# A gated FNet kernel on one core: the last four units of its final product, the sum of its last quarter, one weight of MLP1 and the side jobs of ten MLP1 units in another order

## The chip, the cores and the metric

One core of a Trainium2 chip runs the whole program. The metric is the device time of one execution in microseconds (us), the median of several; lower is better.

## The reference

The input x has 2048 tokens of 512 features; all values are float32.

```
xn  = layernorm(x)                                  # over the 512 features
a,b = xn @ Wd_re^T, xn @ Wd_im^T                    # DFT over the features
s   = Ws_re @ a - Ws_im @ b                         # DFT over the tokens, real part
h   = relu(xn @ w1 + b1) ** 2                       # 512 -> 1792   (MLP1)
g   = silu(h @ w2 + b2)                             # 1792 -> 512   (MLP2)
out = x + s * g
```

## The kernel before

**Arithmetic.** Each float32 matrix is split into a high and a low part (`split`): ScalarE writes the high part as float32r (`split_hi`, L125), VectorE subtracts it from the value and writes the low part (`split_lo`, L128). A product is three matmuls: high by high, high by low, low by high (`PASSES`). Most large products also use a Winograd-Strassen scheme: a 2x2 block product is made of seven products, numbered 1 to 7 (`PRODUCTS`), of sums of blocks. VectorE makes the sums (`sums_b`, L257 to L259; `sums_a`, L263 to L269). "C11, C12, C21, C22" are the four quarters of a result; quarter C21 is the combination that needs product 4 and the sum of the others.

**Stages, in the order of TensorE's queue.** (1) The DFT over the tokens, `PQD = ct^T xn`, in eight chunks of 256 columns, each of eight steps j (L340 for the first two chunks, L325 after). (2) The DFT over the features, eight `YUnit`s (L705), whose operands are read back from DRAM. (3) MLP1, 28 `HUnit`s (L705): unit n has token group c = n // 7 (512 tokens) and weight p = n % 7 (256 hidden features). Its result goes to DRAM (`HD`). (4) MLP2, the units n = 0 to 27 again (`outer`, L811): each adds its share to seven PSUM banks, one for each Strassen product (eight for the last token group, where product 4 has one bank for each half of its columns, `m4[0]` and `m4[1]`). After seven units a token group is combined (`combine`, or by hand for the last group), passed through silu, multiplied by s, added to x and written.

**Order.** Everything is scheduled by hand: each engine runs its instructions in the order in which the program lists them. The work beside the matmuls (loading, summing and splitting operands) is cut into jobs, generators whose next step is issued by `go("name")`. The tables say where: `EARLY[(chunk, step)]` in stage 1, `Y_SIDE` in stage 2, `H_SIDE[n]` in stage 3 with three places in a unit, `O_SIDE` in stage 4. In a unit of stage 3, `before` is the unit ahead of it:

```
go(*first); unit.products(1); seed; before.c11(); before.products(5); before.c22()
before.products(4); before.c21(); go(*second); unit.products(7); unit.m7()
unit.products(6); seed; before.products(3); before.c12(); unit.products(2)
before.square(); go(*later)
```

`c22` and `c21` are on VectorE (L775, or L715 and L718 in the units of `ACT_PAIR`, with L790 after them in the other units), so a job in `first` stands ahead of them on VectorE and one in `second` behind them. Product 3 of a unit is added in the PSUM region that its `c22` has read ("B"), so these matmuls wait for `c22`.

**Jobs by their letters.** V: a weight of MLP1, loaded, summed and split in stages 2 and 3 (`make_w1`, three steps: load, sums, split). v: the same made during stage 1 and written to DRAM (`weight`, four steps: load, sums, then twice split-and-store), for the weights in `W1_EARLY`. k: such a weight read back (`load_w1`, two steps, one for each of the high and low parts, 896 KB each). w: a weight of MLP2 (`make_w2`; load, sums, split). x: a token block (`tokens`), m: its row statistics (`load_rows`). h: an operand of stage 4 (`operand`: load, sums, split). y: an early operand of stage 2 (`y_early`). p: a weight of stage 2 read back (`load_wd`). d: the weights of stage 2 made.

**Buffers that matter here.** `wd0` holds in turn a weight of stage 2, weight 6 of MLP1 (`W1_HOME`) and, in stage 4, the raw operands of every fourth unit. `pq00`, `pq01` are scratch for the v and y jobs with an even number. `u` has three buffers. The split operands of stage 4 rotate over `xc6`, `xc7`, `xc4`.

**The end (L1028 to L1074).** `REST = NP - 3`: the last three units (25, 26, 27) are not added product by product in the loop but kept for the end, where the order of products is chosen so that the quarters of the last token group come ready one after the other. `step` combines a bank with a quarter (L1039), `silu` is ScalarE (L854), `times` multiplies by s (L858), `plus` adds x and issues the store (L863, L864). The last quarter is C21: when the last bank `m4[1]` is complete, `step` subtracts it from the sum of the others, then silu, `times`, `plus` and the store follow. `finish` for an earlier token group may let a GpSimd DMA add x from DRAM (L846), with `put` (L849) as the store.

Of the kernel before, what the change touches and what calls it, by code (L numbers as in the profile page):

```python
# [9 lines left out]
F32R = mybir.dt.float32r  # L10
AF = mybir.ActivationFunctionType
ALU = mybir.AluOpType

P = 128
S, D, F = 2048, 512, 1792
NS, ND, NF = S // P, D // P, F // P
NJ, NP = NS // 2, NF // 2
# [3 lines left out]
NTC = S // TC  # L21
# [2 lines left out]

ASIDE = 4.2

REST = NP - 3

W1_EARLY = (0, 1)
W2_LATE = (4, 5)  # L30


EARLY = {
# [7 lines left out]
}  # L41
# [13 lines left out]

H_SIDE = {
    0: ((), ("V2", "x2"), ("x3",)),
    1: (("V4",), ("V3",), ("V5",)),
    2: ((), ("V4", "V5"), ("V6",)),
    3: ((), ("x3", "V5"), ("m2",)),  # L60
    4: ((), ("V6", "x2"), ("x4",)),
    5: ((), ("V6", "x3"), ("w4",)),
    6: ((), ("x3",), ("x5",)),
    7: (("w4",), ("w4",), ("w5",)),
    8: ((), ("x4",), ()),
# [10 lines left out]
    21: (("h1",), (), ()),  # L76
    22: (("w1",), ("h0",), ("w2",)),
    23: ((), ("h1",), ("w3",)),
    24: (("w2",), ("w1",), ("w6", "h2")),
    25: (("w3",), ("w2",), ("h3", "l4")),  # L80
    26: (("w6",), ("w3",), ("l5",)),
    27: (("h2",), (), ()),
}
ACT_PAIR = (7, 10, 13, 15, 17, 18, 19, 20, 26)
O_SIDE = {0: (("h4",), ("h5",)), 1: ((), ("w6",))}
# [28 lines left out]
C21, C11, C22, C12 = range(4)  # L114
# [5 lines left out]
def fnet_gated_kernel(ctx, tc, x, xt, ct, wd, w1, w2, b1, b2, out):  # L120
    nc = tc.nc
# [27 lines left out]
    WDD = [dram.tile([P, 2, 7, 256], F32, name=f"wdd{n}") for n in range(ND)]  # L149
    W1D = {p: dram.tile([P, 2, 7, 256], F32, name=f"w1d{p}") for p in W1_EARLY}  # L150
    W2D = {p: dram.tile([P, 2, 7, 256], F32, name=f"w2d{p}") for p in W2_LATE}
# [3 lines left out]
    def bank(tag, name):  # L155

        return acc.tile([P, 512], F32, tag=tag, name=name)

    def buf(tag, shape, name, dtype=F32):
        bufs = {"u": 3, "bn": 3, "sm": 3}.get(tag, 1)  # L160
        return pool.tile(shape, dtype, tag=tag, bufs=bufs, name=name)
# [86 lines left out]
    def plain_parts(c, j, hs=slice(0, 2)):  # L248
        if (c, j) not in part:
            part[c, j] = buf("g" + "ab"[j % 2], [P, 2, 4, CW], f"g{c}_{j}", F32R)  # L250
        g, r = part[c, j], raw[c, j]
        s = slice(2 * hs.start, 2 * hs.stop)
        return g[:, HI, s], g[:, LO, s], r[:, s]
# [21 lines left out]
    def sums_w1(t, r):  # L275
        sums_a(t, r[:, 0:1], r[:, 1:4:2], r[:, 1], r[:, 2], turned=True)
# [67 lines left out]
    one, two = slice(0, 1), slice(1, 2)  # L344
# [38 lines left out]

    Y_HOME = ("xc2", "xc3"), ("xc4", "xc5"), ("xc6", "xc7")
    YFIRST = 3
    yop, yraw, WDP = {}, {}, []

    def y_load(n):
        if n < 2 * NC:
# [25 lines left out]

    def load_wd(n):
        t = buf(("wd0", "wd1", "xc0", "xc1")[n], [P, 2, 7, 256], f"wdp{n}", F32R)
        WDP.append(t)
        for i in range(2):
            nc.sync.dma_start(t[:, i].bitcast(F32), WDD[n][:, i])  # L420
            yield
# [35 lines left out]
    g = plain_parts(0, 1)  # L457
# [7 lines left out]
    for j in range(1, NJ):  # L465
# [15 lines left out]
        g = plain_parts(*order[j + 1])  # L481
# [62 lines left out]
    for n, s in enumerate(steps):  # L544
        c, j = s
        if j == 0:
            ms = {k: bank(tag, f"m{k}_{c}") for k, tag in
                  {1: "bb", 2: "b20", 6: "b21", 3: "b30", 5: "b31", 7: "b32", 4: ("ba", "bc")[c % 2]}.items()}
        g = part.pop(s)
# [22 lines left out]
        if j == NJ - 1:  # L572
            e = buf("e", [P, 2048], f"c{c}")
# [9 lines left out]
    xT, W1, W2, fin, ready = {}, {}, {}, {}, {}  # L583
# [52 lines left out]
        yield  # L636

    def make_w1(p):
        e = buf({4: "e", 6: "e"}.get(p, "u"), [P, 8, 256], f"w1raw{p}")
        nc.sync.dma_start(e[:, 0:4], w1[p])  # L640
        yield
        sums_w1(e[:, 4:8], e)
        yield
        t = W1[p] = buf(W1_HOME[p], [P, 2, 7, 256], f"w1_{p}", F32R)
        split(t[:, HI], t[:, LO], e[:, 1:8])
        yield
# [20 lines left out]
    def operand(n):  # L667

        apart = n in (0, 1, 3)
        if apart:  # L670
            x_, t = (buf(f"pq{n % 3}{i}", [P, 4, 256], f"hr{n}_{i}") for i in range(2))
        else:
            e = buf("u" if n % 4 else "wd0", [P, 8, 256], f"hr{n}")
            x_, t = e[:, 4:8], e[:, 0:4]
        nc.sync.dma_start(x_, HD[divmod(n, NP)])
        yield
        sums_rows(t, x_)
        yield
        g = ready[n] = buf(("xc6", "xc7", "xc4")[n % 3], [P, 2, 7, 256], f"g{n}", F32R)
        for s, src in ((slice(0, 4), t), (slice(4, 7), x_[:, 0:3])) if apart else ((slice(0, 7), e[:, 0:7]),):  # L680
            split(g[:, HI, s], g[:, LO, s], src)
        yield
# [122 lines left out]
    def outer(m, k, n, cols=(0, 1)):  # L805

        p = n % NP
        a, b = PRODUCTS[k]
        for i in cols:
            for a_, b_ in PASSES:  # L810
                nc.tensor.matmul(m[:, i * 256:(i + 1) * 256], ready[n][:, a_, H_SLOT[a], i * P:(i + 1) * P],  # L811
                                 W2[p][:, b_, b], start=p == 0 and i == 0 and (a_, b_) == (HI, HI) and k not in BIASED,
                                 stop=p == NP - 1 and (a_, b_) == (LO, HI), skip_group_check=True)
# [22 lines left out]
    def finish(c, e, k):  # L836

        if len(fin[c]) > 2 + k // 2:
            silu(e, k)
            times(c, e, k)  # L840
            plus(c, e, k)
            return
        silu(e, k)
        times(c, e, k)
        z = e[:, k].rearrange("p (k e) -> p k e", e=256)
        nc.gpsimd.dma_start(z, at(x[c * TC:(c + 1) * TC], k), accum_op=ALU.add)  # L846

    def put(c, e, k):
        nc.sync.dma_start(at(out[c * TC:(c + 1) * TC], k), e[:, k].rearrange("p (k e) -> p k e", e=256))  # L849

    def silu(e, k, cols=slice(0, 2)):

        z = e[:, k, cols.start * 256:cols.stop * 256]
        nc.scalar.activation(z, z, AF.Silu)  # L854

    def times(c, e, k, cols=slice(0, 2)):
        w = slice(cols.start * 256, cols.stop * 256)
        nc.vector.tensor_tensor(e[:, k, w], e[:, k, w], fin[c][k // 2][:, k % 2, w], op=ALU.mult)  # L858

    def plus(c, e, k, cols=slice(0, 2), eng=None):  # L860
        w = slice(cols.start * 256, cols.stop * 256)
        z = e[:, k, w]
        (eng or nc.vector).tensor_tensor(z, z, fin[c][2 + k // 2][:, k % 2, w], op=ALU.add)  # L863
        nc.sync.dma_start(at(out[c * TC:(c + 1) * TC], k)[:, cols], z.rearrange("p (k e) -> p k e", e=256))  # L864

    go("m0")
# [23 lines left out]
    for u in range(1, NC):  # L890
        n = 2 * u + 2
# [40 lines left out]
    for n in range(NTC * NP):  # L932
# [17 lines left out]
        if n == NTC * NP - 1:  # L950
            ms = Banks(0)
# [22 lines left out]
    for n in range(NTC * NP):  # L974
        c, p = divmod(n, NP)
        last = c == NTC - 1
        if n and not last and p == 0:

            ms = Banks(c)
            for k in (2, 4, 5):  # L980
                bias(ms[k], k)
        elif last and p == 0:

            ms = {k: bank(t, f"m{k}_last") for k, t in
                  {1: "b20", 2: "b21", 6: "b30", 7: "b31", 5: "bb", 3: "ba"}.items()}
            m4 = bank("bc", "m40_last"), bank("b32", "m41_last")
# [13 lines left out]
        if n == 1:  # L1000
            for k, i in ((1, 1), (2, 1), (6, 1), (4, 1), (5, 0), (3, 0), (7, 1), (5, 1), (3, 1)):
                add(k, i)
        elif n and (not last or p < REST):
            for k in ORDER if p else FIRST_LAST if last else FIRST:
# [7 lines left out]
        if p == NP - 1 and not last:  # L1012
            e = buf("e", [P, 4, 512], f"z{c}")
# [14 lines left out]
    e = buf("u", [P, 4, 512], f"z{c}")  # L1028
    tail = NP - 1
    whole = slice(0, 512)  # L1030
    w = [slice(i * 256, (i + 1) * 256) for i in range(2)]

    def rest(ks, ps=range(REST, NP)):
        for k in ks:
            for f in ps:
                add(k, f)

    def step(to, a, b, op, w=whole):
        nc.vector.tensor_tensor(e[:, to, w], a[:, w], e[:, b, w], op=op)  # L1039

    rest((1, 2, 6), range(REST, tail))
    rest((1, 2), (tail,))
    nc.scalar.activation(e[:, C21], ms[1], AF.Copy)
    step(C11, ms[2], C21, ALU.add)
    silu(e, C11)
    times(c, e, C11)
    plus(c, e, C11)
    rest((6,), (tail,))
    rest((7,))
    step(C12, ms[6], C21, ALU.add)  # L1050
    step(C21, ms[7], C12, ALU.subtract)
    rest((5,))
    step(C22, ms[5], C21, ALU.add)
    silu(e, C22)
    step(C12, ms[5], C12, ALU.subtract)
    rest((3,))
    for f in range(REST, NP):
        outer(m4[0], 4, NP * c + f, (0,))
    times(c, e, C22)
    step(C12, ms[3], C12, ALU.add)  # L1060
    silu(e, C12)
    plus(c, e, C22)
    step(C21, m4[0], C21, ALU.subtract, w[0])
    silu(e, C21, one)
    for f in range(REST, NP):
        outer(m4[1], 4, NP * c + f, (1,))
    times(c, e, C12)
    plus(c, e, C12, eng=nc.gpsimd)
    step(C21, m4[1], C21, ALU.subtract, w[1])
    silu(e, C21, two)  # L1070
    times(c, e, C21, one)
    plus(c, e, C21, one)
    times(c, e, C21, two)
    plus(c, e, C21, two)  # L1074


def _launch(arrays, out_shape):
# [40 lines left out]
```

## Time and profile before

| what | value |
|---|---|
| time, median of 3 runs | 705.61 us (705.03 to 707.03) |
| the profiled execution's own time | 707.13 us |
| its span, first to last instruction | 705.4 us |
| granted TensorE clock in it | 0.998 |
| VectorE (DVE) busy | 606.8 us (86%) |
| ScalarE (ACT) busy | 357.9 us (51%) |
| DMA moved | 146.88 MB, 208 GB/s |

PE is the matmul half of TensorE and PEld its weight loading, DVE is VectorE, ACT ScalarE, POOL GpSimd and SP SyncE, which issues most of the DMAs; DVEq, ACTq and the like are the queues of these engines. A row of the timeline has the start (us from the span's start), the duration, the engine, the line of the kernel, the operation, what it writes and reads, and how many instructions the row merges; in brackets the idle time of the engine before it and what ended it. A row of the waits has the total, the number and the longest wait.

### The profile page before, as it was taken

The page shows a single profiled execution, that of the slowest core. Times are in us where ns is not written, and L with a number is a line of the kernel's source. Part 1 is how long each engine was busy: PE and PEld are TensorE (multiplying, and loading weights), DVE is VectorE, ACT ScalarE, POOL GpSimd, SP SyncE. Part 2 cuts the span into 40 slices and gives each one's busy share as a digit, 9 for nine tenths or more (in the row PEclk, how much of TensorE's full clock was granted, in tenths as well). Part 3 has the DMA queues.
Part 4 walks back from the last instruction along what each step waited for, and adds up shares of the span by engine and source line. Part 5 has one row for each costly group of instructions (what it writes and reads, how often), then busy time and mean ns, then how long its engine had stood idle before and what let it go on. Part 6 is the DMA issues. An engine that isn't in the chain of part 4 may idle for free.

```text
span 705.4 us, 13138 instructions
## 1 busy us (share of the span) xinstructions
PE 695.8 (99%) x5440; PEld 671.7 (95%) x5440; DVE 606.8 (86%) x848; ACT 357.9 (51%) x474; POOL 6.5 (1%) x9
## 2 busy tenths in 40 slices
PE   9999999999999999999999999999999999999996
PEld 6778889999999999999999999999999999999996
DVE  7999779999988988888898699999648599989896
ACT  4446544444434333344455458677778664444441
POOL 0000000000000000000000000000000000101000
PEclk9999999999999999999999999999999999999999
DMA  8535755667475544276587446587426955666743
GB/s 302 190 109 189 269 203 209 247 214 278 174 282 200 184 163 176 94 281 230 176 297 266 151 168 214 204 318 259 157 119 200 356 163 203 185 204 186 235 143 130
DMA packets 50619, 146.88 MB, mean 208 GB/s; under 512 B 4864, under 2 KB 19200, under 8 KB 49152
## 3 DMA queue, kind: packets, MB, share of 16 engines
q1 hardware_dynamic: 43264, 126.13, 51.6%
q10 hardware_dynamic: 6208, 18.88, 6.8%
q0 software_dynamic: 1088, 1.05, 1.0%
q8 instruction: 42, 0.69, 0.4%
q14 instruction: 17, 0.14, 0.1%
HBM read 99.88 MB, written 46.15 MB: 207 GB/s over the span
## 4 chain that ended last, share of the span: by engine, by line
PE 93%; DVE 4%; DMA 1%; ACT 1%; issue 1%; DVEq 0%; ACTq 0%
PE m L325 33%; PE m_o L811 15%; PE r_B L705 12%; PE r_A L705 8%; PE pq_b L340 8%; PE m_last L811 5%; PE r_C L705 4%; PE r_D L705 4%; PE pq_ba L340 2%; PE pq_bb L340 1%; PE pq_bc L340 1%; DMA w2raw<-in_w 1%; DVE c L306 1%; DVE yg L128 0%; DMA x<-in_x 0%
## 5 line engine op out<-in xcount | busy, mean ns | idle before, releaser
L325 PEld LDWEIGHTS m<-g,xc 128*128 128x128 f32 x2016 | 236.4, 188 | 0.5 <-DVE g L128 0.2
L325 PE MATMUL m<-g,xc 128*128 128x256 f32 x2016 | 236.8, 279 | 0.0
L125 ACT ACTIVATE g<-u 128x1792 fp32r<-128x1792 f32 (+3 forms) x70 | 100.1, 1430 | 145.6 <-PE m L325 55.6
L128 DVE TENSOR_TENSOR g<-u,g 128x1792 fp32r<-128x1792 f32 (+3 forms) x70 | 117.5, 1679 | 27.0 <-ACT g L125 26.8
L811 PE MATMUL m_o<-w,g 128*128 128x256 f32 x882 | 105.8, 282 | 0.0
L811 PEld LDWEIGHTS m_o<-w,g 128*128 128x128 f32 x882 | 105.5, 191 | 0.0
L125 ACT ACTIVATE g<-hr 128x1792 fp32r<-128x1792 f32 (+2 forms) x31 | 47.9, 1556 | 49.5 <-PE m_o L811 31.4
L705 PE MATMUL r_B<-xT,w 128*128 128x256 f32 x504 | 70.3, 283 | 0.8 <-DVE h L775 0.8
L340 PE MATMUL pq_b<-g,xc 128*128 128x512 f32 x240 | 66.8, 397 | 0.2
L705 PEld LDWEIGHTS r_B<-xT,w 128*128 128x128 f32 x504 | 64.4, 190 | 1.4 <-DVE h L775 1.1
L128 DVE TENSOR_TENSOR g<-hr,g 128x1792 fp32r<-128x1792 f32 (+2 forms) x31 | 56.8, 1839 | 7.9 <-ACT g L125 7.9
L340 PEld LDWEIGHTS pq_b<-g,xc 128*128 128x128 f32 x240 | 43.8, 188 | 13.2 <-ACT xc L125 2.3
L705 PE MATMUL r_A<-xT,w 128*128 128x256 f32 x336 | 45.0, 282 | 1.3 <-DVE w L128 1.3
L705 PEld LDWEIGHTS r_A<-xT,w 128*128 128x128 f32 x336 | 42.1, 190 | 1.5 <-DVE w L128 1.5
L705 PE MATMUL r_B<-wdp,yg 128*128 128x256 f32 x288 | 37.5, 283 | 0.2 <-DVE y L715 0.2
L705 PEld LDWEIGHTS r_B<-wdp,yg 128*128 128x128 f32 x288 | 35.6, 190 | 0.6 <-DVE y L715 0.4
L811 PE MATMUL m_last<-w,g 128*128 128x256 f32 x294 | 35.3, 282 | 0.0
L811 PEld LDWEIGHTS m_last<-w,g 128*128 128x128 f32 x294 | 35.2, 191 | 0.0
L257 DVE TENSOR_TENSOR u<-u 128x512 f32<-128x512 f32 x48 | 32.9, 685 | 1.9 <-DMA u<-in_ct 1.9
L128 DVE TENSOR_TENSOR yg<-yraw,yg 128x1792 fp32r<-128x1792 f32 x13 | 26.2, 2020 | 3.8 <-ACT yg L125 3.8
L306 DVE TENSOR_TENSOR c<-m,c 128x512 f32<-128x512 f32 x42 | 27.2, 685 | 1.7 <-PE m L325 1.0
L125 ACT ACTIVATE yg<-yraw 128x1792 fp32r<-128x1792 f32 x13 | 22.1, 1697 | 6.6 <-DVE yraw L266 5.2
(172 smaller groups left out, 865.4 us busy)
## 6 DMA issues: line engine op xcount, KB each, us to landing
u<-in_ct SPq DMA_DIRECT2D x63, 512.0 KB, 3.6
hd<-h ACTq DMA_DIRECT2D x28, 512.0 KB, 4.1
hr<-hd SPq DMA_DIRECT2D x28, 512.0 KB, 3.7
wdp<-wdd SPq DMA_DIRECT2D x8, 896.0 KB, 6.5
yraw<-pqd SPq DMA_DIRECT2D x13, 512.0 KB, 5.1
pqd<-c SPq DMA_DIRECT2D x6, 1024.0 KB, 4.0
y<-y ACTq DMA_DIRECT2D x8, 512.0 KB, 4.3
fin<-y SPq DMA_DIRECT2D x16, 256.0 KB, 5.1
```

The source lines that it names most:

```text
L125: nc.scalar.activation(hi, src, AF.Copy)
L128: nc.vector.tensor_tensor(lo, src, hi.bitcast(F32), op=ALU.subtract)
L257: nc.vector.tensor_tensor(t[:, 0:2], r[:, 0:1].to_broadcast([P, 2, 256]), r[:, 1:3], op=ALU.add)
L306: nc.vector.tensor_tensor(part_(to), m, part_(frm), op=op)
L325: nc.tensor.matmul(ps[:, d], w[:, a_, d * P:(d + 1) * P], halves(mv(b_)), start=first and d == 0 and (a_, b_) == (HI, HI), stop=last and ( ...
L340: nc.tensor.matmul(accs[c][k], w, part[c, j][:, b_, 2 * h:2 * h + 2], start=j == 0 and h == 0 and (a_, b_) == (HI, HI), stop=j == NJ - 1 a ...
L705: nc.tensor.matmul(self.region(REGION[k]), w, mv, start=i == 0 and k in (1, 7), stop=i == len(ops) - 1, skip_group_check=True)
L811: nc.tensor.matmul(m[:, i * 256:(i + 1) * 256], ready[n][:, a_, H_SLOT[a], i * P:(i + 1) * P], W2[p][:, b_, b], start=p == 0 and i == 0 an ...
```

## The change

The program computes the same. Six things move:

- Weight 6 of MLP1 joins `W1_EARLY`: it is made in chunks 3 and 4 of stage 1 by the job v6 (its load takes the place of that of y0), stored to DRAM, and read back by k6 in units 1 and 2. The job V6 is gone from units 2, 4 and 5. In chunks 4 and 5 the jobs y0, y1, p0 and p1 are placed differently; `WDP` is filled by index, since p1 now comes before p0.
- In units 3, 4 and 5 the jobs of x3, m2 and w4 are re-laid.
- In units 24 to 27 what stood in `first` stands in `second`, and two of the `second` jobs of a unit stand in one list.
- Four units, not three, are kept for the end. Their order is: products 1, 2, 6, 7, 5 of units 24 and 25; products 1, 2 of 26, then of 27; 6, 7 of both; 5 of both; 3 of all four; then product 4 of all four, one half of the columns after the other. Unit 27's operand goes to `wd0`.
- The sum of the other products for C21 is subtracted in PSUM from `m4[0]` and `m4[1]` ahead of their last matmuls, so silu reads the bank itself when it is complete.
- In the last token group x is added to C11 by a GpSimd DMA (`add_x`) and stored by `put`; C12 gets its x on VectorE instead of GpSimd.

```
-REST = NP - 3
-W1_EARLY = (0, 1)
+REST = NP - 4
+W1_EARLY = (0, 1, 6)
 EARLY:
-    (3, 5): ("v0", "y0"), (3, 6): ("v1",),
-    (4, 2): ("v1",), (4, 3): ("v1", "y1"), (4, 5): ("p0",), (4, 6): ("p0",), (5, 2): ("y0",), (5, 3): ("p1",),
-    (5, 4): ("y1",), (5, 5): ("p1",),
+    (3, 5): ("v0", "v6"), (3, 6): ("v1",),
+    (4, 2): ("v1",), (4, 3): ("v1", "y1"), (4, 4): ("v6",), (4, 5): ("v6",), (4, 6): ("v6", "y0"),
+    (5, 2): ("p1",), (5, 3): ("p1",), (5, 4): ("y0",), (5, 5): ("p0",), (5, 6): ("p0", "y1"),
 H_SIDE:
-    1: (("V4",), ("V3",), ("V5",)),
-    2: ((), ("V4", "V5"), ("V6",)),
-    3: ((), ("x3", "V5"), ("m2",)),
-    4: ((), ("V6", "x2"), ("x4",)),
-    5: ((), ("V6", "x3"), ("w4",)),
+    1: (("V4",), ("V3",), ("V5", "k6")),
+    2: ((), ("V4", "V5"), ("k6",)),
+    3: ((), ("V5",), ("w4",)),
+    4: ((), ("x2", "x3", "m2"), ("x4",)),
+    5: ((), ("x3",), ()),
...
-    24: (("w2",), ("w1",), ("w6", "h2")),
-    25: (("w3",), ("w2",), ("h3", "l4")),
-    26: (("w6",), ("w3",), ("l5",)),
-    27: (("h2",), (), ()),
+    24: ((), ("w1", "w2"), ("w6", "h2")),
+    25: ((), ("w2", "w3"), ("h3", "l4")),
+    26: ((), ("w3", "w6"), ("l5",)),
+    27: ((), ("h2",), ()),
...
-        g = ready[n] = buf(("xc6", "xc7", "xc4")[n % 3], ...)
+        g = ready[n] = buf("wd0" if n == NTC * NP - 1 else ("xc6", "xc7", "xc4")[n % 3], ...)
...
+    def add_x(c, e, k):
         z = e[:, k].rearrange("p (k e) -> p k e", e=256)
         nc.gpsimd.dma_start(z, at(x[c * TC:(c + 1) * TC], k), accum_op=ALU.add)
...
-    rest((1, 2, 6), range(REST, tail))
+    for f in range(REST, tail - 1):
+        rest((1, 2, 6, 7, 5), (f,))
+    rest((1, 2), (tail - 1,))
     rest((1, 2), (tail,))
     nc.scalar.activation(e[:, C21], ms[1], AF.Copy)
     step(C11, ms[2], C21, ALU.add)
     silu(e, C11)
+    for f in (tail - 1, tail):
+        rest((6, 7), (f,))
+    step(C12, ms[6], C21, ALU.add)
     times(c, e, C11)
-    plus(c, e, C11)
-    rest((6,), (tail,))
-    rest((7,))
-    step(C12, ms[6], C21, ALU.add)
+    add_x(c, e, C11)
     step(C21, ms[7], C12, ALU.subtract)
-    rest((5,))
+    rest((5,), (tail - 1, tail))
+    for i in range(2):
+        nc.vector.tensor_tensor(m4[i][:, w[i]], m4[i][:, w[i]], e[:, C21, w[i]], op=ALU.subtract)
     step(C22, ms[5], C21, ALU.add)
     silu(e, C22)
     step(C12, ms[5], C12, ALU.subtract)
+    times(c, e, C22)
+    plus(c, e, C22)
     rest((3,))
-    for f in range(REST, NP):
-        outer(m4[0], 4, NP * c + f, (0,))
-    times(c, e, C22)
+    put(c, e, C11)
     step(C12, ms[3], C12, ALU.add)
     silu(e, C12)
-    plus(c, e, C22)
-    step(C21, m4[0], C21, ALU.subtract, w[0])
-    silu(e, C21, one)
-    for f in range(REST, NP):
-        outer(m4[1], 4, NP * c + f, (1,))
     times(c, e, C12)
-    plus(c, e, C12, eng=nc.gpsimd)
-    step(C21, m4[1], C21, ALU.subtract, w[1])
-    silu(e, C21, two)
-    times(c, e, C21, one)
-    plus(c, e, C21, one)
-    times(c, e, C21, two)
-    plus(c, e, C21, two)
+    plus(c, e, C12)
+    for i, part_ in enumerate((one, two)):
+        for f in range(REST, NP):
+            outer(m4[i], 4, NP * c + f, (i,))
+        nc.scalar.activation(e[:, C21, w[i]], m4[i][:, w[i]], AF.Silu)
+        times(c, e, C21, part_)
+        plus(c, e, C21, part_)
```

More of the change, by code (lines that the diff above doesn't have):

```diff
@@ L385, in fnet_gated_kernel @@
     YFIRST = 3
-    yop, yraw, WDP = {}, {}, []
+    yop, yraw, WDP = {}, {}, {}
     def y_load(n):
@@ L417, in load_wd @@
         t = buf(("wd0", "wd1", "xc0", "xc1")[n], [P, 2, 7, 256], f"wdp{n}", F32R)
-        WDP.append(t)
+        WDP[n] = t
         for i in range(2):
@@ L638, in make_w1 @@
     def make_w1(p):
-        e = buf({4: "e", 6: "e"}.get(p, "u"), [P, 8, 256], f"w1raw{p}")
+        e = buf("e" if p == 4 else "u", [P, 8, 256], f"w1raw{p}")
         nc.sync.dma_start(e[:, 0:4], w1[p])
@@ L678, in operand @@
         yield
-        g = ready[n] = buf(("xc6", "xc7", "xc4")[n % 3], [P, 2, 7, 256], f"g{n}", F32R)
+        g = ready[n] = buf("wd0" if n == NTC * NP - 1 else ("xc6", "xc7", "xc4")[n % 3], [P, 2, 7, 256], f"g{n}", F32R)
         for s, src in ((slice(0, 4), t), (slice(4, 7), x_[:, 0:3])) if apart else ((slice(0, 7), e[:, 0:7]),):
@@ L844, in finish @@
         times(c, e, k)
+        add_x(c, e, k)
+    def add_x(c, e, k):
         z = e[:, k].rearrange("p (k e) -> p k e", e=256)
@@ L858, in times, with plus @@
         nc.vector.tensor_tensor(e[:, k, w], e[:, k, w], fin[c][k // 2][:, k % 2, w], op=ALU.mult)
-    def plus(c, e, k, cols=slice(0, 2), eng=None):
+    def plus(c, e, k, cols=slice(0, 2)):
         w = slice(cols.start * 256, cols.stop * 256)
         z = e[:, k, w]
-        (eng or nc.vector).tensor_tensor(z, z, fin[c][2 + k // 2][:, k % 2, w], op=ALU.add)
+        nc.vector.tensor_tensor(z, z, fin[c][2 + k // 2][:, k % 2, w], op=ALU.add)
         nc.sync.dma_start(at(out[c * TC:(c + 1) * TC], k)[:, cols], z.rearrange("p (k e) -> p k e", e=256))
```

2 rows, old and new, of the table EARLY are left out of this document.

## The prediction

> **What bounds the kernel now.** I read the totals first, then who TensorE waited for.
>
> ```profile
> span 705.4 us, 13138 instructions
> PE 695.8 (99%) x5440; PEld 671.7 (95%) x5440; DVE 606.8 (86%) x848; ACT 357.9 (51%) x474; POOL 6.5 (1%) x9
> ...
> PE r_A L705 <- DVE w L128: 1.3, 1, 1.3
> ...
> PE r_B L705 <- DVE h L775: 0.8, 1, 0.8
> PE r_B L705 <- DVE y L715: 0.2, 1, 0.2
> ```
>
> PE is busy for 695.8 of 705.4 us. The change takes away no matmul, so 695.8 us stay, and all that can be won lies in the 9.6 us beside them: the start, two waits within the work (1.3 and 0.8 us; the 0.2 us wait belongs to stage 2, which the change leaves), and what follows the last matmul. So I looked for each of these in the timeline and asked whether the change touches it, and then whether the moved work opens a new gap.
>
> **First gap: weight 6 of MLP1.** The timeline at the start of unit 6:
>
> ```profile
> 441.39 1.77 PE L705 MATMUL r_B<-xT,w 128*128 128x256 f32 x12
> 443.00 1.11 PE L705 MATMUL r_A<-xT,w 128*128 128x256 f32 x8
> 443.36 2.02 DVE L128 TENSOR_TENSOR w<-w1raw,w 128x1792 fp32r<-128x1792 f32 x1
> 445.43 0.74 PE L705 MATMUL r_A<-xT,w 128*128 128x256 f32 x4 [1.32 <-DVE w L128]
> ```
>
> Six of the eight r_A matmuls are product 2 of unit 5, two are the first of unit 6; the next ones wait for the low part of weight 6, which V6 finishes at 445.38. Eight matmuls at 0.12 us each (the rate of the 294-matmul row below) would end at 443.96, so the gap is 445.43 - 443.96 = 1.5 us. After the change V6 is not there. Its stand-in k6 is two transfers:
>
> ```profile
> w<-w1d SPq DMA_DIRECT2D x4, 896.0 KB, 8.9
> ...
> 421.70 7.59 SPq L640 DMA_DIRECT2D w1raw<-in_w  x2
> ```
>
> The first of these two issues (421.7) is V5's load; k6's first half stands right behind it and the second half a unit later without a wait, since the wait for V4 that held SP until 429 (421.70 + 7.59) belongs to V6's load. Even one after the other at 8.9 us each they land by 422 + 17.8 = 440, before 443.7 when unit 6 starts. **1.5 us are won.** If SP were held until 429 as now, the second half would land up to 3 us after unit 6 starts; then this gain would be lost.
>
> The re-laid x3 (row below: its two subtract/multiply instructions, 2.48 us) goes from unit 3 to unit 4. DVE then has, over units 3 and 4, 1.5 us less than before (V6's sums are gone) but more of it in unit 4, and it may idle in between.
>
> ```profile
> 432.08 2.48 DVE L610 TENSOR_TENSOR xr<-xr,rows 128x1024 f32<-128x1024 f32 x2
> ```
>
> The two effects about cancel, so c22 of unit 5 gets its turn no later than now; it is a little late now, since the twelve r_B matmuls of 441.39 (above) take 1.77 us where 1.58 is usual (row of 533.10 below). That 0.2 us stays. I count the re-laying at nothing, with a gain of 0.2 and a loss of 0.5 as bounds (all of the idling in unit 4 lost, against nothing of it).
>
> **Second gap: units 24 to 26.**
>
> ```profile
> 533.10 1.58 PE L705 MATMUL r_B<-xT,w 128*128 128x256 f32 x12
> 537.69 0.69 DVE L257 TENSOR_TENSOR w2raw<-w2raw 128x512 f32<-128x512 f32 x1 [1.89 <-DMA w2raw<-in_w]
> 538.11 0.88 PE L705 MATMUL r_B<-xT,w 128*128 128x256 f32 x6
> 539.22 0.48 DVE L775 SCALAR_TENSOR_TENSOR h<-r_B,b1s,h 128x256 f32<-128x256 f32 x1
> 539.75 0.98 PE L705 MATMUL r_B<-xT,w 128*128 128x256 f32 x6 [0.76 <-DVE h L775]
> 540.92 2.02 DVE L128 TENSOR_TENSOR w<-w2raw,w 128x1792 fp32r<-128x1792 f32 x1
> ...
> 544.16 1.73 PE L705 MATMUL r_B<-xT,w 128*128 128x256 f32 x12
> 549.33 1.81 PE L705 MATMUL r_B<-xT,w 128*128 128x256 f32 x12
> 554.53 1.77 PE L705 MATMUL r_B<-xT,w 128*128 128x256 f32 x12
> ```
>
> DVE stands at the sums of w2 (`first` of unit 24) until their DMA lands; c22 is queued behind them, and product 3 behind c22. The gap is 539.75 - 538.11 - 6 x 0.12 = 0.9 us. The three following units lose 0.15, 0.23 and 0.19 us against the 1.58 us of an undisturbed row, in the same place: sums ahead of c22. With everything in `second`, c22 comes first. DVE's load of a unit becomes c22, c21, L790 (0.48 + 0.48 + 0.69), a split (2.02) and sums (0.68 + 2 x 0.42): 5.2 us against a unit of 5.0, so each of three units starts 0.2 us later than the one before, 0.6 in all. Between product 5, which c22 reads, and product 3, which waits for it, stand products 4, 7 and 6: 18 matmuls, 2.2 us, of which c22 takes 0.48. It has 1.7 us to spare, and 0.6 is less: nothing new is late. **0.9 + 0.5 = 1.4 us are won**, bounds 0.9 to 1.5.
>
> **The tail.**
>
> ```profile
> 660.91 4.72 DVE L306 TENSOR_TENSOR z<-m_o,z 128x512 f32<-128x512 f32 x7 [1.20 <-PE m_o L811]
> 664.25 35.25 PE L811 MATMUL m_last<-w,g 128*128 128x256 f32 x294
> 686.21 2.03 DVE L128 TENSOR_TENSOR g<-hr,g 128x1792 fp32r<-128x1792 f32 x1 [0.84 <-ACT g L125]
> 698.11 0.63 ACT L854 ACTIVATE z<-z 128x512 f32<-128x512 f32 x1 [1.52 <-DVE z L1039]
> 699.54 0.43 DVE L1039 TENSOR_TENSOR z<-m_last,z 128x256 f32<-128x256 f32 x1
> 699.70 1.26 POOL L863 TENSOR_TENSOR z<-z,fin 128x512 f32<-128x512 f32 x1 [56.62 <-DVE z L858]
> 699.88 1.35 DVE L858 TENSOR_TENSOR z<-z,fin 128x256 f32<-128x256 f32 x1
> 700.00 0.42 ACT L854 ACTIVATE z<-z 128x256 f32<-128x256 f32 x1 [0.54 <-DVE z L1039]
> ...
> 702.07 0.42 DVE L863 TENSOR_TENSOR z<-z,fin 128x256 f32<-128x256 f32 x1
> ```
>
> TensorE ends at T = 699.50, the last `plus` at 702.49, the span at 705.4: 3.0 us of vector work and 2.9 us for the last store and the end of the program. In the 3.0 us lie the subtraction from the bank (0.43) and a `times` of 256 columns that took 1.35 us instead of 0.42 while POOL added x for C12. Both go. But the change also moves work of DVE towards the end, so I count DVE's queue on from the moment product 6 is complete, in matmuls before T: 48 for product 4 and 3, 12 for 5, 6 for the last 7, so 66 x 0.12 = T - 7.9. From there it has, before the silu of C12, eight instructions of 512 columns (0.67 each, from the run of seven) and the two new subtractions in PSUM (0.45 each): 6.3 us, to T - 1.6; the inputs of each are there (product 5 at T - 5.8, product 3 at T - 2.9, the silus of 0.63 in between). Then silu of C12 with the handovers, 0.7: T - 0.9. `times` and `plus` of C12, 1.3: T + 0.4. `times` and `plus` of the two halves, 4 x 0.42: T + 2.1; the silu of the last half, 0.42 after T, is done long before its turn. So 3.0 becomes 2.1, and **0.9 us are won**. Upper bound: were DVE not behind, silu, `times`, `plus` would end at T + 1.4, a gain of 1.6. Lower bound: nothing, if the subtractions into PSUM cost more than those out of it (no row shows a DVE write to PSUM) or the queue runs 0.9 us later.
>
> Two covers must hold. The subtractions in PSUM end at about T - 4.9 in this count, and the first matmul of product 4's kept part comes at T - 2.9: 2 us to spare. Unit 27's operand is needed 96 matmuls before T now, at T - 11.5, not 90; its low part ended at 688.24 = T - 11.3, but DVE stood idle for 0.84 us before it, since its buffer was held by unit 24. With `wd0` that wait is gone, T - 12.1: 0.6 us to spare.
>
> `add_x` and `put` for C11 replace a `plus` of 0.67. What they cost is read from the same DMA for the earlier token groups, the issue and the line's landing times:
>
> ```profile
> 641.85 1.23 POOL L846 DMA_DIRECT2D z<-in_x  x1 [3.76 <-DVE z L858]
> DMA to landing us min/median/max: 4.6/5.0/5.3
> ...
> out<-z SPq DMA_DIRECT2D x15, 256.0 KB, 3.7
> ...
> out<-z SPq DMA_DIRECT2D x2, 128.0 KB, 1.8
> ```
>
> C11's `times` ends at T - 6.5; POOL 1.2, landing 5.0: x is added by T - 0.3. SP stands at `put` until then; queued behind it is only C12's store, due at T + 0.4. `put` then lands by T + 0.1 + 3.7 = T + 3.8. The last half leaves DVE at T + 2.1 and ends the span 2.9 us later, at T + 5.0; of these 2.9 its landing takes 1.8, the issue 0.4, the program's end the other 0.7. So `put` is done 0.5 us before it decides (T + 3.8 + 0.7 against T + 5.0); what it is later than that counts in full.
>
> **Made earlier: v6.** The job costs DVE sums and a split in two pieces in steps 4 to 6 of chunk 4, at the price of v1's rows, and there DVE idles:
>
> ```profile
> 171.16 0.68 DVE L263 TENSOR_TENSOR w11t<-w11r 128x512 f32<-128x512 f32 x1
> 191.44 0.95 DVE L128 TENSOR_TENSOR w11g<-w11r,w11g 128x768 fp32r<-128x768 f32 x1
> 195.84 1.22 DVE L128 TENSOR_TENSOR w11g<-w11t,w11g 128x1024 fp32r<-128x1024 f32 x1
> ...
> 203.69 2.02 DVE L128 TENSOR_TENSOR g<-u,g 128x1792 fp32r<-128x1792 f32 x1 [1.35 <-ACT g L125]
> 208.59 2.02 DVE L128 TENSOR_TENSOR g<-u,g 128x1792 fp32r<-128x1792 f32 x1 [0.95 <-ACT g L125]
> 213.49 2.03 DVE L128 TENSOR_TENSOR g<-u,g 128x1792 fp32r<-128x1792 f32 x1 [1.35 <-ACT g L125]
> ```
>
> Sums 0.68 + 2 x 0.42 = 1.5, pieces 0.95 and 1.22, each of which falls into one of these idle times (1.35, 0.95, 1.35): the worst is 0.2 us late, and takes from the next. The two stores (1024 and 768 KB) take the places of the two 896 KB reads of p0 in SP's queue. Nothing is lost, bounds 0 to 0.4.
>
> **The sum.** 1.5 + 1.4 + 0.9 = 3.8 us. The profiled execution took 707.13 us, 1.7 more than its span and 1.5 above the median of the runs, 705.61; it would become 703.3, and the median 705.61 - 3.8 = **701.8 us**.
>
> **The rivals.** *The tail wins nothing* (its lower bound): 1.5 + 1.4 = 2.9, 702.7 us. For it: DVE is the last to end either way, and its count is a sum of 15 instructions. Against: the 0.93 us lost to POOL are certain to go.
>
> *The gaps only move.* V6 out, but x3 in unit 4 or the three sums in `second` make c22 late again by as much. Then only the tail counts: 704.7 us, no change that can be told. For it: DVE's load of 5.2 us in a unit of 5.0. Against: 0.6 us of drift with 1.5 to spare.
>
> *Slower: the DMA that adds x starves.* It decides when POOL cannot write its descriptors while DVE is at work. After C11's `times` DVE's only pause is the 0.7 us of C12's silu, shorter than POOL's 1.23, so the DMA would start at T + 2.1, end POOL's part at 3.3, land at 8.3, and `put` (0.4 and 3.7, and 0.7 for the program's end) would end the span at T + 13.1 instead of T + 5.9: +7.2 - 2.9 = 4.3 us slower, 709.9. Against it: at 641.85 POOL took 1.23 us as always, though DVE was working then.
>
> The Trainium skill (SBUF — State Buffer, § Who interferes with whom) warns of this: a DMA issued by GpSimd gets its descriptors from GpSimd's cores, which DVE can lock out of a port pair they share. By the same section a `tensor_tensor` like those of this tail takes only the read side of the pair and leaves descriptor writing free, and the row at 641.85 agrees.
>
> **How the numbers follow.** The forecast 0.70; the tail wins nothing 0.15; the gaps only move 0.08; slower 0.07. A measurement of this kernel tells a change from none beyond about 0.3%, 2.1 us. Faster by more than that: 0.70 + 0.15 = 0.85; within: 0.08; slower: 0.07. The range: downwards the tail's upper bound (0.7 more) and 0.6 for the scatter of the medians (the runs lie 2.0 us apart), 700.5; upwards to the case of the gaps that only move, 704.7, which leaves out the slower case and some of the edges.
>
> **What would show it.** Right: the waits of PE have no row for L128 in stage 3 and none, or under 0.3 us, for L775; the twelve r_B matmuls of units 24 to 27 take 1.58; the last `plus` ends some 2.1 us after the last matmul; POOL's only row near the end is the DMA, 1.2 us long; no PE gap opens in chunks 4 and 5. Wrong: a wait of r_A for a DMA of w at unit 6; a new gap at unit 5, at stage 1, or before the last units' operands; a `put` that lands last.

## The result and the profile after

The changed kernel takes 702.36 us (median of 6 runs, 701.73 to 702.93) against 705.88 us for the kernel before (6 runs, 704.86 to 707.03): a ratio of 0.9948, 95% interval 0.9934 to 0.9961, 3.5 us less. The forecast was 701.8 us, 3.8 us less. The profiled execution took 701.75 us with a span of 700.0; the one before 707.13 with 705.4. The two profiles are thus 5.4 us apart, 1.9 more than the medians, and why is the main finding below.

The page after, first the totals, then who TensorE waited for:

```profile
span 700.0 us, 13144 instructions
PE 693.0 (99%) x5440; PEld 670.1 (96%) x5440; DVE 605.6 (87%) x849; ACT 357.9 (51%) x475; POOL 6.4 (1%) x9
...
PE warm L443 <- DVE idle L439: 1.2, 1, 1.2
PE pq_b L340 <- ACT xc L125: 1.0, 1, 1.0
PE r_B L705 <- DVE y L715: 0.2, 1, 0.2
```

Both waits of stage 3 (1.3 and 0.8 us before) are gone. The 1.0 us at pq_b lies ahead of the first product, at 7.7 us, which the change leaves as it was; where it shows in the profiles of this study it is 0.4 to 1.6 us long. It moves little: the matmuls of L325 start 97.9 to 98.2 us into the span in all fourteen profiles, with this wait or without it.

The timeline at units 5 and 6, where V6 was:

```profile
440.76 1.60 PE L705 MATMUL r_B<-xT,w 128*128 128x256 f32 x12
442.20 1.59 PE L705 MATMUL r_A<-xT,w 128*128 128x256 f32 x12
443.63 0.87 PE L705 MATMUL r_B<-xT,w 128*128 128x256 f32 x6
```

The twelve r_A run through, and the twelve r_B ahead of them take 1.60 instead of 1.77. Lined up matmul by matmul, the two profiles move apart by 1.75 us here: the 1.5 us of the gap and the 0.2 us of unit 5, which the prediction had left standing.

Units 24 and 25:

```profile
534.55 0.48 DVE L775 SCALAR_TENSOR_TENSOR h<-r_B,b1s,h 128x256 f32<-128x256 f32 x1 [1.14 <-PE r_B L705]
536.33 2.02 DVE L128 TENSOR_TENSOR w<-w2raw,w 128x1792 fp32r<-128x1792 f32 x1
538.27 0.68 DVE L257 TENSOR_TENSOR w2raw<-w2raw 128x512 f32<-128x512 f32 x1
...
540.76 1.60 PE L705 MATMUL r_B<-xT,w 128*128 128x256 f32 x12
```

DVE now does c22 first (534.55) and the sums of w2 last (538.27), and the r_B row is undisturbed. Here the profiles move apart by 1.54 us.

The end:

```profile
660.32 35.15 PE L811 MATMUL m_last<-w,g 128*128 128x256 f32 x294
689.36 1.21 POOL L849 DMA_DIRECT2D z<-in_x  x1 [50.10 <-DVE z L861]
689.58 0.76 DVE L1059 TENSOR_TENSOR m_last<-m_last,z 128x256 f32<-128x256 f32 x2
692.97 0.69 DVE L1042 TENSOR_TENSOR z<-m_last,z 128x512 f32<-128x512 f32 x1
694.35 0.69 DVE L861 TENSOR_TENSOR z<-z,fin 128x512 f32<-128x512 f32 x1 [0.70 <-ACT z L857]
695.50 0.38 ACT L1074 ACTIVATE z<-m_last 128x256 f32<-128x256 f32 x1 [0.91 <-PE m_last L811]
696.93 0.42 DVE L866 TENSOR_TENSOR z<-z,fin 128x256 f32<-128x256 f32 x1
```

The last matmul ends at 695.47, the last `plus` at 697.35: 1.9 us instead of 3.0. The two subtractions into PSUM take 0.38 us each. DVE idles once, for the 0.70 us of C12's silu, and is otherwise at work until the end. The silu of the last half is done at 695.88, 0.6 us before its `times` (696.48): VectorE's queue decides the end, not the chain behind the last bank.

The span ends 4.51 us after the last matmul instead of 5.85, which is 1.34 of the 5.4 us. Most of what is left, 0.6 us, lies in stage 1, where no wait was taken away: its 1986 matmuls ran for 233.13 us in the profile of before (first row) and for 232.60 in that of the changed kernel (second row).

```profile
98.16 233.13 PE m L325 x1986
```
```profile
98.06 232.60 PE m L325 x1986
```

This is scatter between executions and no gain: in six other profiles of kernels whose stage 1 is that of the changed kernel, the same row reads 232.91 to 233.88.

### The profile page after: what moved, and what is told of

Its sections match the earlier page's. It is cut to its first block, busy times and chain, and to the rows that moved or that the text cites. A ratio compares the mean times of both kernels' runs of the same rounds, so it can differ in the third digit from the quotient of the medians.

```text
span 700.0 us, 13144 instructions
## 1 busy us (share of the span) xinstructions
PE 693.0 (99%) x5440; PEld 670.1 (96%) x5440; DVE 605.6 (87%) x849; ACT 357.9 (51%) x475; POOL 6.4 (1%) x9
## 4 chain that ended last, share of the span: by engine, by line
PE 94%; DVE 3%; DMA 1%; ACT 1%; issue 1%; SPq 0%; DVEq 0%; ACTq 0%
PE m L325 33%; PE m_o L811 15%; PE r_B L705 13%; PE r_A L705 8%; PE pq_b L340 8%; PE r_C L705 4%; PE r_D L705 4%; PE m_last L811 4%; PE pq_ba L340 2%; PE pq_bc L340 1%; PE pq_bb L340 1%; DMA rows<-rows 1%; DVE yg L128 0%; DMA x<-in_x 0%; DVE bn L185 0%
## 5 line engine op out<-in xcount | busy, mean ns | idle before, releaser
L325 PEld LDWEIGHTS m<-g,xc 128*128 128x128 f32 x2016 | 235.7, 188 | 0.6 <-DVE g L128 0.2
L325 PE MATMUL m<-g,xc 128*128 128x256 f32 x2016 | 236.2, 280 | 0.0
```

What stands on the lines that cost most here:

```text
L325: nc.tensor.matmul(ps[:, d], w[:, a_, d * P:(d + 1) * P], halves(mv(b_)), start=first and d == 0 and (a_, b_) == (HI, HI), stop=last and ( ...
```

## The experiments

**Each part of the change by itself, added to the kernel before.**

```
only_v6:     W1_EARLY, EARLY, WDP, H_SIDE[1..5], make_w1 as changed; the rest as before
only_24_27:  H_SIDE[24..27] as changed; the rest as before
only_tail:   REST, operand, add_x and everything from L1041 on as changed; the rest as before
```

> The kernel before, with weight 6 of MLP1 made in stage 1 and read back, and units 1 to 5 re-laid; nothing else of the change. If the three parts are independent (theory), the row of r_A waiting for L128 is gone, the wait of r_B for L775 at unit 24 (0.8 us) stays, no new wait appears, TensorE ends 1.5 to 1.8 us earlier and the time falls by about 1.7 us, to 0.9976 of before. If the gap only moves (rival), unit 5's c22 or unit 24's wait grows by as much and the time is that of before.

> The kernel before, with units 24 to 27 re-laid alone. Theory: the r_B wait for L775 is gone, the twelve r_B matmuls of units 25 to 27 take 1.6 instead of 1.73 to 1.81 us, the 1.3 us wait at unit 6 stays; TensorE ends 1.4 to 1.6 us earlier, 0.9978 of before. Rival: the three sums behind c22 make it late again (DVE has 5.2 us of work in units of 5.0), less than 0.5 us is won.

> The kernel before, with the four kept units, their order, the sum in PSUM, the DMA for C11's x and unit 27's buffer, and nothing else. Theory: TensorE ends when it did (699.5 of a span of 705.4, give or take the scatter of its rate), the last plus ends 1.9 us after it instead of 3.0 and the span 4.5 to 4.7 us after it instead of 5.9: 1.3 us less, 0.998 of before. Rival (the tail wins nothing by itself, and what the changed kernel showed there came from stages before it): 5.9 us as before.

| kernel | ratio to before, 95% | times, us |
|---|---|---|
| only_v6 | 0.9986 (0.9976 to 0.9996) | 703.65 to 706.03, 12 runs |
| only_24_27 | 0.9995 (0.9987 to 1.0004) | 705.23 to 706.11, 12 runs |
| only_tail | 0.9984 (0.9974 to 0.9993) | 703.99 to 706.16, 12 runs |
| before, beside them | 1 | 705.06 to 708.08, 29 runs |

The first and third went as expected in the trace as far as their own part goes: with v6 alone TensorE's wait at unit 6 is gone and the matmuls behind it are 1.72 us earlier; with the tail alone the last `plus` ends 1.9 us after the last matmul. In the time only_v6 fell short: its median is 0.8 us less than that of before (704.93 against 705.75), where 1.7 was expected. Four of its 12 runs, the profiled one among them, lie at 703.65 to 704.22, where 1.7 us less would be, and eight at 704.77 to 706.03; why is not shown. The three ratios add up to 0.35% less, where the whole change gives 0.52%, but the intervals are too wide to tell these apart. The second part won next to nothing, where 1.4 to 1.6 us were expected, and the traces of the other two say why. TensorE's waits in only_tail, whose units 24 to 27 are those of the kernel before:

```profile
PE pq_b L340 <- ACT xc L125: 1.3, 1, 1.3
PE r_A L705 <- DVE w L128: 1.3, 1, 1.3
PE warm L443 <- DVE idle L439: 1.2, 1, 1.2
PE r_B L705 <- DVE y L715: 0.2, 1, 0.2
```

The wait for L775 is not there, though nothing was done to it; nor is it in only_v6, where it was expected to stay. DVE came to the sums of w2 and did not have to stand (only_tail, timeline; the first row begins with the issue of w2's load):

```profile
531.57 10.12 SPq L654 DMA_DIRECT2D w2raw<-in_w  x3
536.09 0.68 DVE L257 TENSOR_TENSOR w2raw<-w2raw 128x512 f32<-128x512 f32 x1
537.61 0.48 DVE L775 SCALAR_TENSOR_TENSOR h<-r_B,b1s,h 128x256 f32<-128x256 f32 x1
```

The load was issued at 531.57, so it took 4.5 us at most; in the profile of before it took 6.5, by its chain of work:

```profile
531.20 6.46 DMA w2raw<-in_w
```

The rows of units 25 to 27, where the prediction saw 0.15 to 0.23 us lost to sums ahead of c22, run through in 1.60 in only_tail, with the sums still ahead: that loss too came with the late load. The second gap, which the prediction took for a part of the kernel, belongs to executions in which the load lands late. The times fit: of the 29 runs of before in this set, 21 lie between 705.06 and 705.88 and 8 between 706.55 and 708.08, and the profiled one, at 707.13, is of the upper kind. In the other three sets the two kinds are less clean, with 5 of 41 runs between 705.98 and 706.27. only_24_27 has no run above 706.11.

Of the fourteen profiles of this study, the load lands 4.3 to 4.4 us after its issue in ten and, apart from the two kernels below that delay it, late in two: the kernel before (6.5) and c22_plus_later (6.5), a kernel with units 24 to 27 as changed. There TensorE has no wait at unit 24, so the new order takes up a late load that nobody forced.

**The late load on purpose.** One more 512 KB read ahead of w2's load, in the kernel before and in the changed one:

```
 def make_w2(p):
+        if p == 2:
+            nc.sync.dma_start(t, w2[p])
         nc.sync.dma_start(r, w2[p])
```

> The kernel before, with one more read of 512 KB (w2's raw weight, into the scratch half that the sums overwrite later) ahead of w2's own load in unit 22, so that the load lands later. Theory: the gap of units 24 to 27 in the profile of before belongs to executions in which w2's load lands late (6.5 us after its issue; 4.5 us or less in the kernels where the gap was absent); here it is late in every execution, L775 stops TensorE for 0.5 to 1.5 us at unit 24 and all times lie above 706.5. Rival (the gap comes from the sums themselves standing ahead of c22, whenever they land): no more than now, 705.8.

> The changed kernel with the same additional read ahead of w2's load. Theory: the sums stand behind c22, so the late landing reaches nothing: no row of r_B waiting for L775, the time is the changed kernel's within 0.3 us. Rival: the late landing pushes the sums into unit 25's c22 and 0.5 us or more is lost.

before_late took 707.84 us (707.03 to 709.22, 12 runs), a ratio of 1.0025 (1.0015 to 1.0036): every run lies at or above 707, where only the upper kind lay. Its timeline at unit 24 (the lines are 2 further down, as the edit adds two):

```profile
538.27 0.69 DVE L257 TENSOR_TENSOR w2raw<-w2raw 128x512 f32<-128x512 f32 x1 [2.70 <-DMA w2raw<-in_w]
...
540.33 0.98 PE L707 MATMUL r_B<-xT,w 128*128 128x256 f32 x6 [1.58 <-DVE h L777]
```

DVE stands 2.7 us for the load, c22 behind it, TensorE 1.6 us behind c22. after_late took 702.96 us, 0.9952 (0.9938 to 0.9967): the changed kernel's ratio, though 0.6 us above its median, where 0.3 was expected. Its trace has no wait of TensorE at unit 24; against the changed kernel's profile its matmuls lose nothing from stage 3 on (the 0.8 us that its last matmul is behind arise earlier, where both kernels are the same). So the re-laying of units 24 to 27 takes away a loss that comes in some executions. That all runs above 706.5 are such executions is likely but not shown: one of them was profiled, and the scatter of stage 1 (up to 1.3 us, above) can add to a time as well.

**Re-laying units 3 to 5, apart from V6's leaving.**

```
-    3: ((), ("V5",), ("w4",)),  4: ((), ("x2", "x3", "m2"), ("x4",)),  5: ((), ("x3",), ()),
+    3: ((), ("x3", "V5"), ("m2",)),  4: ((), ("x2",), ("x4",)),  5: ((), ("x3",), ("w4",)),
```

> The changed kernel with x3, m2 and w4 of units 3 to 5 at their old places, V6 still gone. Theory: V6's leaving is what counts; c22 of unit 4 was just in time before and stays so, unit 5's is no longer late, so no wait appears and TensorE ends when the changed kernel's does. Rival: the re-laying was needed, and r_B waits for L775 0.2 us or more in units 4 to 6.

702.18 us, 0.9942 (0.9926 to 0.9959), and no wait in stage 3: the new places of x3, m2 and w4 are worth nothing by themselves. V6's leaving is what counts.

**v6 where VectorE has no room.**

```
-    (4, 4): ("v6",), (4, 5): ("v6",), (4, 6): ("v6", "y0"),
+    (4, 4): ("v6", "v6", "v6"), (4, 6): ("y0",),
```

> The changed kernel with all three VectorE steps of v6 (3.7 us) in step 4 of chunk 4, instead of one in each of steps 4 to 6. Theory: the steps are free because each fits into an idle time of VectorE of 0.95 to 1.35 us; together they do not, the split for step 6 ends about 1.5 us after its matmuls could start, and a wait of m for L128 of 1 to 2 us appears in chunk 4. Rival: VectorE is far enough ahead of TensorE, and nothing changes.

704.20 us, 0.9977 (0.9967 to 0.9987). This is 1.8 us more than the changed kernel. The split for step 6 (206.14) ends at 208.16, and TensorE waits for it:

```profile
206.14 2.02 DVE L128 TENSOR_TENSOR g<-u,g 128x1792 fp32r<-128x1792 f32 x1
...
208.21 4.01 PE L325 MATMUL m<-g,xc 128*128 128x256 f32 x32 [1.33 <-DVE g L128]
```

In the changed kernel, with one step of v6 in each of three steps, the same splits still wait for ScalarE (idle 0.41 and 0.22 us where it was 0.95 and 1.35 before), so VectorE has caught up by then:

```profile
205.30 0.95 DVE L128 TENSOR_TENSOR w16g<-w16r,w16g 128x768 fp32r<-128x768 f32 x1
208.18 2.02 DVE L128 TENSOR_TENSOR g<-u,g 128x1792 fp32r<-128x1792 f32 x1 [0.41 <-ACT g L125]
213.08 2.03 DVE L128 TENSOR_TENSOR g<-u,g 128x1792 fp32r<-128x1792 f32 x1 [0.22 <-ACT g L125]
```

**The tail, one piece at a time, from the changed kernel.**

```
c11_plus:        -    add_x(c, e, C11)  ...  put(c, e, C11)      +    plus(c, e, C11)
no_psum_sum:     the two subtractions in PSUM left out;
                 +    step(C21, m4[i], C21, ALU.subtract, w[i]); silu(e, C21, half)   behind each bank
                 (the second pair behind times and plus of C12)
c12_pool:        -    plus(c, e, C12)      +    plus(c, e, C12, eng=nc.gpsimd)
rest3:           -REST = NP - 4            +REST = NP - 3
c22_plus_later:  plus(c, e, C22) behind step(C12, ms[3], C12, ALU.add), put(c, e, C11) behind times(c, e, C12)
```

> The changed kernel, but C11 gets its x by a plus on VectorE with its own store, as before the change, in place of the GpSimd DMA and the later store. If VectorE's queue decides the end (theory), its 0.6 to 0.7 us comes ahead of everything behind it: the last plus ends 2.5 us after TensorE instead of 1.9, the span is 0.6 us longer than the changed kernel's. If the queue has room before product 3 (rival), nothing changes, and if the GpSimd DMA or the store behind it was what the end waited for (second rival), the end comes earlier.

> The changed kernel without the two subtractions in PSUM: C21's halves are combined after the bank is complete, as before the change (step, silu, times, plus), the order of VectorE's last instructions as before the change. Theory (VectorE's queue decides the end): the two subtractions come back behind the last matmuls, the last plus ends 2.5 us after TensorE instead of 1.9, span 0.6 us longer. Rival (their place does not matter, since VectorE does as many instructions): 1.9 us as now.

> The changed kernel with C12's x added by GpSimd again, as before the change. Theory: GpSimd's 1.26 us and VectorE's times of the first half, both reading two tensors of SBUF, cannot run together: that times takes 1.3 us or more instead of 0.42, VectorE saves a plus of 0.69, and the last plus ends 2.2 to 2.5 us after TensorE instead of 1.9. Rival: what VectorE is spared outweighs it, 1.5 us or less.

> The changed kernel with three units kept for the end instead of four (unit 24 goes product by product in the loop), the new order otherwise. Theory: the fourth unit hides nothing that decides; unit 27's operand has its own buffer and is in time, and the order of the last 96 matmuls is the same, so TensorE has no new wait, the last plus still ends 1.9 us after it, and the time is the changed kernel's. Rival: the operands of units 25 to 27 are late without it, and a wait of m_last for L128 of 0.3 us or more appears.

> The changed kernel with C22's plus moved behind the step that completes C12, so that it runs while ScalarE makes C12's silu and VectorE would stand idle (0.7 us), and the store of C11 one place later in SP's queue. Theory (VectorE's queue decides the end): the last plus ends 0.3 to 0.4 us sooner, 1.5 us after TensorE, and the span is 0.3 us shorter. Rival (the stores decide): no change, or longer.

| kernel | last plus after the last matmul | span's end after it | time, us | ratio to before, 95% |
|---|---|---|---|---|
| before | 3.0 | 5.9 | 705.88 | 1 |
| changed | 1.89 | 4.5 | 702.36 | 0.9948 (0.9934 to 0.9961) |
| c11_plus | 2.62 | 5.2 | 703.36 | 0.9960 (0.9946 to 0.9975) |
| no_psum_sum | 2.28 | 4.9 | 702.73 | 0.9951 (0.9937 to 0.9965) |
| c12_pool | 2.12 | 4.9 | 703.02 | 0.9960 (0.9946 to 0.9974) |
| rest3 | 3.34 | 6.0 | 704.01 | 0.9973 (0.9963 to 0.9983) |
| c22_plus_later | 1.58 | 4.2 | 702.17 | 0.9949 (0.9935 to 0.9962) |

The times resolve little below 1 us, and the span's end scatters too: in five profiles with the changed kernel's tail (changed, only_tail, x3_in_3, v6_one_step, after_late) it comes 4.5 to 4.9 us after the last matmul. The last `plus` comes 1.89 to 1.90 us after it in all five, so the verdicts rest on that column. c11_plus and c22_plus_later went as the queue of VectorE says: an instruction of 0.7 us more ahead of C12's silu ends everything 0.73 us later, one that fills the idle time of that silu 0.31 us sooner. no_psum_sum cost 0.39, not 0.6. c12_pool cost 0.23, a little under its bounds: the collision is there, but it hit a `plus`, after the `times` of the first half had slipped through:

```profile
695.73 1.37 POOL L866 TENSOR_TENSOR z<-z,fin 128x512 f32<-128x512 f32 x1 [4.56 <-DVE z L861]
696.02 1.37 DVE L866 TENSOR_TENSOR z<-z,fin 128x256 f32<-128x256 f32 x1
```

1.37 us for an instruction that takes 0.42 alone. The Trainium skill (SBUF — State Buffer, § Who interferes with whom) has it so: the second of a GpSimd instruction that reads SBUF and a VectorE instruction with two SBUF inputs blocks until the first is done. The rows agree: the `plus` ends at 697.39, just behind POOL's instruction, which ends at 697.10.

**rest3 was the miss.** It was expected to change nothing, and the last `plus` came 1.45 us later:

```profile
687.78 8.48 PE L811 MATMUL m_last<-w,g 128*128 128x256 f32 x70
...
689.88 0.69 DVE L1042 TENSOR_TENSOR z<-m_last,z 128x512 f32<-128x512 f32 x1 [1.39 <-PE m_last L811]
695.20 0.68 DVE L1042 TENSOR_TENSOR z<-m_last,z 128x512 f32<-128x512 f32 x1
699.16 0.42 DVE L866 TENSOR_TENSOR z<-z,fin 128x256 f32<-128x256 f32 x1
```

Matmuls end at 696.26, no operand was late. But VectorE's queue starts when product 6 is complete (step C12, 689.88), and from there to the end TensorE has 12 matmuls fewer with three kept units: 6 of product 3 and 6 of product 4. 12 x 0.12 = 1.44 us. The queue itself is as long as before, 9.70 us from 689.88 to 699.58, as in the changed kernel from 687.66 to 697.35. What the fourth unit buys is matmuls for VectorE's queue to hide behind; without it the last `plus` comes later after the last matmul than in the kernel before (3.34 us against 3.0).

## Why the prediction was right, and where not

The total, -3.8 us against -3.5, and the direction were right. That it came so near is in part luck: the largest error, a gap counted in full that most executions seem not to have, was partly made up by two terms that turned out larger.

- **Weight 6, 1.5 us:** measured 1.7 to 1.75. The mechanism was right. The 0.2 us of unit 5 that "stays" went too: unit 5's c22 came at 440.74, in time, since VectorE had no sums of V6 in unit 4. Both halves of k6 were issued at 421.5 and never waited for.
- **Units 24 to 26, 1.4 us:** this step failed. The gap was real in the trace, its chain (load, sums, c22, product 3) is what before_late shows, and the re-laying does remove it. But it was counted in full against a median that mostly does not have it. Done alone it moved the time by 0.05%, within its interval of no change; the 1.54 us appear where the profile of before, with its late load, is one of the two. (The three losses of 0.15, 0.23 and 0.19 also add up to 0.57, not to the 0.5 that was counted.) The prediction had the hint: the profiled execution took 1.5 us more than the median, almost the gap's own length, and the load's 6.5 us stood beside a median of 5.0 for that kind.
- **The tail, 0.9 us:** mis-sized. The last `plus` came 1.1 us earlier after the last matmul (1.89 where 2.1 was counted: the subtractions took 0.38 instead of 0.45, and the queue runs in 0.64 a step where nothing waits); the span's end, 1.34 us between the two profiles, 1.1 in only_tail: what lies behind the last `plus` scatters between 2.6 and 3.0 us with one and the same tail. The way of counting was right, the queue's length against the matmuls left; but the fourth unit's 12 matmuls stood in that sum (66 instead of 54) without being named as what the gain hangs on.
- **Put together:** 1.75 and 1.1 to 1.3 come to about 3.0, and the gap of units 24 to 26 in part of the runs adds some tenths; 3.5 was measured, with an interval of 2.8 to 4.7. The rest is inside the scatter.
- **Covers:** unit 27's operand, the subtractions and k6 were in time (no wait of TensorE for any of them). `put` was issued at 693.70 and did not land last: it took 2.3 us, where 3.7 was counted.
- **Rivals:** the gaps did not move, though VectorE's c22 in units 25 to 27 came 5.2 us apart, as the rival had it (539.79, 545.02, 550.26): no row of product 3 took over 1.60 us. The DMA that adds x was not starved: POOL's 689.36 row is 1.21 us long with VectorE at work throughout.

## What to carry to other kernels

One profiled execution shows gaps of the kernel and gaps of that execution; before a gap is counted, compare the profiled time with the median, and if the releaser is a DMA, its landing time with others of its kind. In an in-order queue a job that waits for a load belongs behind the instructions that TensorE waits for, even if the load is usually in time. When a queue of another engine ends last, count it from its first release to the end: matmuls moved behind that release shorten the end as surely as instructions taken away.

## What was not expected of the hardware

The same 512 KB load, in the same place of the same queue, landed 4.3 to 4.4 us after its issue in ten profiles and after 6.5 in two (the kernel before and c22_plus_later). In both late ones a store of 512 KB that ScalarE's queue issues 0.2 us behind the load was late as well, 6.4 and 6.5 us against 5.3 to 5.5 in the ten; what delayed both is open. TensorE's stream in stage 1, without a wait that the profile shows, took 232.60 to 233.88 us for the same 1986 matmuls in seven profiles of kernels with the same stage 1. The granted clock does not explain it: its mean over the execution was 0.998 in the fastest of these executions (the changed kernel) and 1.000 in the slowest (c11_plus).
